# Moving a softmax's sums and scaling from ahead of one elementwise product to behind it, in two chunks of a fused attention and SwiGLU kernel

## The chip, the cores and the metric

The kernel runs on one core of one Trainium2 chip. The metric is the device time of one execution in microseconds (us). One execution was also profiled, and its trace is what the working below is read from. The engines are called as in the profile: PE (TensorE, matmuls; PEld are its weight loads), DVE (VectorE), ACT (ScalarE), POOL (GpSimd) and SP (SyncE, which issues the DMAs).

## The reference

A small set of 32 learned queries `p` packs keys and values of 576 tokens per head; the tokens' queries `q` then attend to the 32 packed rows; a SwiGLU layer follows. There are 8 batch elements, 8 heads, and a head dimension of 64.

```
def sm_attn(qq, kk, vv):
    s = scale * np.matmul(qq, kk.transpose(0, 1, 3, 2))
    s = s - np.max(s, axis=-1, keepdims=True)
    a = np.exp(s)
    a = a / (np.sum(a, axis=-1, keepdims=True) + 1e-09)
    return np.matmul(a, vv)
p_packed = sm_attn(p, k, v)
out = sm_attn(q, p_packed, p_packed)
...
g = x @ w_gate
silu = g * (1.0 / (1.0 + np.exp(-g)))
val = x @ w_val
return (silu * val @ w_out).astype(np.float32)
```

`x` is the attention's output as 4608 tokens of 512 numbers; `w_gate` and `w_val` are 512 by 1536, `w_out` is 1536 by 512. "The second softmax" below is the one of the second `sm_attn`, over 32 packed rows for every token.

## The kernel before

The eight batch elements (called batches, 0 to 7) go through the SwiGLU layer one after the other. Batch 0 follows a written-out list of words; batches 1 to 7 run the loop at L828, and the change touches that loop alone. In it, a batch is twelve **chunks** `fc` = 0 to 11 of 128 hidden units each, and a chunk has two halves of tokens, a (256 wide) and b (320 wide).

For each half, PE computes gate and value into two PSUM banks named `gv` (`gv_chunk`, 6 matmuls each, L558). ACT then takes the SiLU of the gate bank into `sg` (L565), and DVE multiplies it with the value bank into `hf` (L569); in half b a second, narrow product goes into `t4` (L572, shown as `t` in the profile). Products are kept at full precision by splitting each into a high and a low word: ACT copies `hf` to its high word `hh` (L105, in `h_split`), and DVE subtracts to get the low word `hl` (L539). In the following chunk PE multiplies `hl` and `hh` with `w_out` into four accumulators `acc` (`outs`, L577). After every second chunk, 16 further matmuls (`m_part`, L195) prepare the next pair of chunks' weights in two banks named `aux`; ACT copies them to `mh` (L524) and DVE subtracts to get `ml` (L498).

The `gv` pool has two PSUM banks. So the gate matmuls of a half may start when ACT has read the gate bank of the half before, and the value matmuls when DVE has finished both `hf` and `t4` of the half before.

In between these, a batch does the attention of the next batch `d`. `plan_of` says where: `at(fc, place, ...)` puts a step at a place of chunk `fc`. Of a chunk, place "a" lies behind the SiLU of half a, "ha" and "hb" lie between the `hh` copy and the `hl` subtraction of half a and half b, and the numbers 2, 4 and 8 count PE's groups: 2 is behind half a's gate and value matmuls, 4 behind the `outs` that follow (so ahead of half b), 8 at the chunk's end. The second softmax is done in two parts, one in chunks 7 to 9 and one in chunks 9 to 11. Each goes through these steps:

- `s2_mm`: 16 matmuls of scores (L195) into two banks that it takes from the `gv` pool as well (named `gv_aux`), and `s2_block`: two transposes out of them by DVE (L438), at place "ha" of chunk 7 and of chunk 9
- `s2_max`: maximum and subtraction by DVE (L452, L453), at the end of chunk 7 and of chunk 9
- `s2_exp`: exponential by ACT (L457), which needs a table load, and whose next SiLU needs another
- `s2_sums` (L464 to L466) and `s2_scale` (L470): sum, a small addition, reciprocal and a product, by DVE. These are what the change moves
- `s2_turn`: a transpose back by DVE (L479), at the end of chunk 8 and of chunk 10; `s2_high`: ACT's copy to the high word `a2h` (L482); `s2_low`: DVE's low word `a2l` (L486), at place 4 of chunk 9 and of chunk 11

PE's order is the written one. On DVE and ACT the compiler's scheduler settles the order, except that the instructions passed through `pin` keep their written order among each other. Batch 7 has no next batch, so the steps of the plan are run in six batches, 1 to 6.

Of the kernel before, what the change touches and what calls it, by code (L numbers as in the profile page):

```python
# [59 lines left out]
def tile_pack_attention_swiglu(ctx: ExitStack, tc: tile.TileContext, qT, kT, v, vq, pT, wgv, wout, out):  # L60
# [30 lines left out]
    def pin(ins):  # L91

        return tc.keep_in_program_order(ins) if steady[0] else ins
# [71 lines left out]
    def load_k(b):  # L165
        p_t = pool.tile([P, NHP, NP], F32, tag="p", bufs=2, name="p_t")
        (nc.sync if b else nc.scalar).dma_start(p_t, pT[b])
        k_t = io_tile(0, [P, 2, NHP, HS], F32, "k_t")
        if b == 0:
            qs[b] = io_tile(0, [P, 2, NHP, HS], F32, "q_t")  # L170
        for hf in range(2):
            nc.sync.dma_start(k_t[:, hf], kT[b, :, hf])
        kps[b] = (k_t, p_t)
# [135 lines left out]
    def q_scores(b, g, bank=ps):  # L309


        k_t, p_t = kps[b]
        if g == 0:
            e = pool.tile([P, NPAR, NHP, NKQ * NP], F32, tag="s2", bufs=1, name="e1")
            z = pool.tile([P, 2, NPAR, NHP], F32, tag="z1", bufs=2, name="z1")
            sq[b] = [e, z]
            nc.gpsimd.memset(e[:, :, :, SQ:], 0.0)
        e, z = sq[b]
        pss = [bank(), bank()]
        for i in range(2):  # L320
            for j in range(NJ):
                for par in range(NPAR):
                    r = slice(64 * par, 64 * par + 64)
                    nc.tensor.matmul(
                        pss[par][NP * j : NP * j + NP, i * SQ : (i + 1) * SQ],
                        p_t[r, 2 * g + i, :],
                        k_t[r, j // 2, 2 * g + i, j % 2 * SQ : j % 2 * SQ + SQ],
                        start=True, stop=True,
                    )
        sc[b, g] = pss  # L330

    def q_read(b, g, pars):

        e, z = sq[b]
        pss = sc[b, g]
        hs = slice(2 * g, 2 * g + 2)
        for par in pars:
            x, m = pss[par][:, : 2 * SQ].rearrange("p (h n) -> p h n", h=2), z[:, 0, par, hs]
            pin(nc.vector.tensor_reduce(m, x, axis=AX.X, op=ALU.max))
            pin(nc.vector.tensor_tensor(  # L340
                e[:, par, hs, :SQ], x, m.unsqueeze(2).broadcast_to([P, 2, SQ]), op=ALU.subtract
            ))

    def q_exp(b, g):
        x = sq[b][0][:, :, 2 * g : 2 * g + 2, :SQ]
        pin(nc.scalar.activation(x, x, AF.Exp, scale=SCALE))

    def q_sums(b, g):
        e, z = sq[b]
        hs = slice(2 * g, 2 * g + 2)  # L350
        pin(nc.vector.tensor_reduce(z[:, 1, :, hs], e[:, :, hs, :SQ], axis=AX.X, op=ALU.add))

    def q_gather(b):

        x = pool.tile([P, NJ, 2, H], F32, tag="x1", bufs=1, name="x1")
        zd = dram.tile([P, 2, H], F32, tag="zd", bufs=2, name="zd")
        nc.sync.dma_start(zd, sq[b][1].rearrange("p s r h -> p s (r h)"))
        for i in range(NJ):
            nc.sync.dma_start(x[NP * i : NP * i + NP], zd.rearrange("(j n) s h -> n j s h", j=NJ))
        sq[b].append(x)  # L360

    def q_common(b):

        _, z, x = sq[b]
        y = pool.tile([P, 3, NJ + 1, H], F32, tag="pp", bufs=1, name="y1")
        sq[b].append(y)
        m = y[:, 2, 0]
        pin(nc.vector.tensor_reduce(m, x[:, :, 0].rearrange("p j h -> p h j"), axis=AX.X, op=ALU.max))
        pin(nc.vector.tensor_tensor(
            y[:, 0, :NJ], x[:, :, 0], m.unsqueeze(1).broadcast_to([P, NJ, H]), op=ALU.subtract  # L370
        ))
        pin(nc.vector.tensor_tensor(y[:, 0, NJ], z.rearrange("p s r h -> p s (r h)")[:, 0], m, op=ALU.subtract))

    def q_common_exp(b):
        y = sq[b][3]
        pin(nc.scalar.activation(y[:, 0], y[:, 0], AF.Exp, scale=SCALE))

    def q_factors(b):

        _, _, x, y = sq[b]  # L380
        t, f = y[:, 2, 1], y[:, 2, 2]
        pin(nc.vector.tensor_tensor(y[:, 1, :NJ], y[:, 0, :NJ], x[:, :, 1], op=ALU.mult))
        pin(nc.vector.tensor_reduce(t, y[:, 1, :NJ].rearrange("p j h -> p h j"), axis=AX.X, op=ALU.add))
        pin(nc.vector.tensor_scalar(f, t, 1e-9, None, op0=ALU.add))
        pin(nc.vector.reciprocal(t, f))
        pin(nc.vector.tensor_tensor(f, t, y[:, 0, NJ], op=ALU.mult))

    def q_turn(b, par):
        e, f = sq[b][0], sq[b][3][:, 2, 2]
        if par == 0:  # L390
            sq[b].append(pool.tile([P, NPAR, NHP, NKQ, NP], F32, tag="a1", bufs=1, name="a1"))
        w = e[:, par, :, :SQ]
        pin(nc.vector.tensor_tensor(
            w, w, f[:, NHP * par : NHP * par + NHP].unsqueeze(2).broadcast_to([P, NHP, SQ]), op=ALU.mult
        ))
        pin(nc.vector.transpose(
            sq[b][4][:, par].rearrange("p h k n -> p (h k n)"), e[:, par].rearrange("p h n -> p (h n)")
        ))
# [41 lines left out]
    def s2_view(b, cs):  # L440
        s2, r2 = st2[b]
        n = NPAR * NBK
        rows = slice(cs.start * n, cs.stop * n)
        return (
            s2[:, cs].rearrange("p c r (k n) -> p (c r k) n", n=NP),
            [r2[:, i, rows] for i in range(3)],
            [P, (cs.stop - cs.start) * n, NP],
        )
# [13 lines left out]
    def s2_sums(b, cs):  # L462
        x, (m, s, r), _ = s2_view(b, cs)
        pin(nc.vector.tensor_reduce(s, x, axis=AX.X, op=ALU.add))  # L464
        pin(nc.vector.tensor_scalar(m, s, 1e-9, None, op0=ALU.add))
        pin(nc.vector.reciprocal(r, m))  # L466

    def s2_scale(b, cs):
        x, (_, _, r), shape = s2_view(b, cs)
        pin(nc.vector.tensor_tensor(x, x, r.unsqueeze(2).broadcast_to(shape), op=ALU.mult))  # L470
# [121 lines left out]
    def plan_of(b):  # L592

        d, plan = b + 1, {}

        def at(fc, place, *todo):
            plan.setdefault((fc, place), []).extend(todo)  # L600

        if d < B:
            c, c2 = (1, 0) if d % 2 else (0, 1)
            cs, cs2 = slice(c, c + 1), slice(c2, c2 + 1)
            at(0, 2, lambda: q_scores(d, 0))
            at(0, "ha", lambda: q_read(d, 0, (0,)))
            at(0, "hb", lambda: q_read(d, 0, (1,)))
            at(1, "a", lambda: q_exp(d, 0))
            at(1, "ha", lambda: q_scores(d, 1, gv_ps), lambda: q_read(d, 1, (0, 1)))
            at(1, 8, lambda: q_sums(d, 0))  # L610
            at(2, "a", lambda: q_exp(d, 1))
            at(2, 8, lambda: q_sums(d, 1), lambda: q_gather(d))
            at(3, 8, lambda: q_common(d))
            if d + 1 < B:
                at(3, 8, lambda: load_k(d + 1))
            at(4, "a", lambda: q_common_exp(d))
            at(4, 4, lambda: q_factors(d))
            at(4, 8, lambda: q_turn(d, 0))
            at(5, 8, lambda: q_turn(d, 1))
            at(6, 4, lambda: q_pack(d, 0))  # L620
            at(6, 8, lambda: q_pack(d, 1))
            if d + 1 < B:
                at(7, "ha", lambda: load_v(d + 1))
            at(7, "ha", lambda: s2_tiles(d), lambda: s2_a2(d))
            at(7, "ha", lambda: s2_mm(d, c, gv_ps), lambda: s2_block(d, c))
            at(7, 8, lambda: s2_max(d, cs))
            at(8, "a", lambda: s2_exp(d, cs))
            at(8, 4, lambda: s2_sums(d, cs), lambda: s2_scale(d, cs))
            at(8, 8, lambda: s2_turn(d, c), lambda: s2_high(d, c))
            at(9, "ha", lambda: s2_mm(d, c2, gv_ps), lambda: s2_block(d, c2))  # L630
            if d + 1 < B:
                at(9, "ha", lambda: load_q(d + 1))
            at(9, 4, lambda: s2_low(d, c))
            at(9, 8, lambda: s2_max(d, cs2))
            at(10, "a", lambda: s2_exp(d, cs2))
            at(10, 4, lambda: s2_sums(d, cs2), lambda: s2_scale(d, cs2))
            at(10, 8, lambda: s2_turn(d, c2), lambda: s2_high(d, c2))
            at(11, 4, lambda: s2_low(d, c2))
        return lambda fc, place: bool([f() for f in plan.pop((fc, place), ())])

    with tc.manual_schedule(engines={mybir.EngineType.PE}):
# [186 lines left out]
        for b in range(1, B):  # L828
            rows, accs = begin(b)
            run = plan_of(b)  # L830
            ha, hb = {}, {}
# [80 lines left out]
```

## Time and profile before

| what | value |
|---|---|
| time, median of 3 runs (lowest to highest) | 749.33 us (749.03 to 750.16) |
| time of the profiled execution | 749.33 us |
| its span, from the first to the last instruction | 747.5 us |
| busy in the span: PE / DVE / ACT | 736.2 / 455.4 / 367.9 us |
| idle of PE before its `gv` matmuls for `t` of DVE | 1.8 us in 7 waits |
| mean granted PE clock, as a share of full | 0.998 |

The span leaves out 1.8 us of the execution's own time. Busy time of an engine counts overlapping instructions once; PE's matmuls are pipelined, so that one's listed duration reaches into the next ones, and the distance between two starts tells more than a duration. A wait in the profile is idle time of one engine together with the instruction of another engine that ended it.

### The profile page before, as it was taken

The numbers are of one execution on the slowest core, as the hardware profiler recorded it, in microseconds if no ns is written. First come the engines' busy times: TensorE is split into PE (matmuls) and PEld (weight loads), VectorE is DVE, ScalarE is ACT, GpSimd is POOL, SyncE is SP. The second block draws the span as 40 slices with busy tenths as digits, with TensorE's granted clock in tenths as the row PEclk, the third lists the DMA queues.
The fourth block names the chain that finished last, engine by engine and source line by source line (L and its number), as shares of the span: only waits on it lengthen the run. The fifth ranks groups of instructions, "written<-read, shape, count | busy, mean of one in ns | idle before, by whom it ended". The sixth has DMA issues, their size and how long they took to land.

```text
span 747.5 us, 15126 instructions
## 1 busy us (share of the span) xinstructions
PE 736.2 (98%) x6280; PEld 594.8 (80%) x6280; DVE 455.4 (61%) x1004; ACT 367.9 (49%) x662; POOL 2.0 (0%) x13
## 2 busy tenths in 40 slices
PE   7999999999999999999999999999999999999998
PEld 4756666888788887887888888888888888888886
DVE  5988878665756557645765556655575555744334
ACT  3777745754516445563544535464452644533331
POOL 0000000000000000000000000000000000000000
PEclk9999999999999999999999999999999999999999
DMA  9686583202112021302112022100201000010001
GB/s 354 251 313 249 182 323 114 72 3 72 64 71 69 2 72 65 124 4 72 64 57 83 3 72 64 58 3 1 72 2 71 3 1 2 1 57 1 1 1 71
DMA packets 20004, 59.15 MB, mean 79 GB/s; under 512 B 5984, under 2 KB 7008, under 8 KB 17376
## 3 DMA queue, kind: packets, MB, share of 16 engines
q1 hardware_dynamic: 19792, 58.12, 21.5%
q8 instruction: 49, 0.80, 0.5%
q14 instruction: 19, 0.16, 0.1%
q10 hardware_dynamic: 144, 0.07, 0.0%
HBM read 48.69 MB, written 9.49 MB: 78 GB/s over the span
## 4 chain that ended last, share of the span: by engine, by line
PE 90%; DVE 4%; ACT 2%; issue 1%; DVEq 0%; ACTq 0%
PE gv L558 34%; PE acc L577 29%; PE aux L195 7%; PE gv L742 6%; PE acc L768 6%; PE aux L577 4%; PE aux L410 1%; ACT L457 1%; PE gv_aux L195 1%; PE acc L646 1%; DVE hf L569 1%; PE warm_ps L646 1%; DVE hl L539 1%; DVE s L453 1%; ACT hh L105 1%
## 5 line engine op out<-in xcount | busy, mean ns | idle before, releaser
L565 ACT ACTIVATE sg<-gv 128x256 f32<-128x256 f32 (+1 forms) x168 | 68.9, 410 | 166.0 <-PE gv L558 134.7
L558 PE MATMUL gv<-a2h,ml 128*128 128x256 f32 (+1 forms) x672 | 147.2, 300 | 2.3 <-DVE t L572 1.8
L569 DVE TENSOR_TENSOR hf<-gv,sg 128x256 f32<-128x256 f32 x168 | 70.7, 421 | 121.2 <-PE gv L558 99.1
L558 PE MATMUL gv<-a2h,mh 128*128 128x256 f32 (+1 forms) x672 | 144.2, 296 | 0.0
L558 PE MATMUL gv<-a2l,mh 128*128 128x256 f32 (+1 forms) x672 | 144.0, 296 | 0.0
L577 PE MATMUL acc<-wo_h,hl 128*128 128x512 f32 x336 | 136.2, 405 | 0.0
L577 PE MATMUL acc<-wo_l,hh 128*128 128x512 f32 x336 | 132.2, 393 | 0.0
L577 PE MATMUL acc<-wo_h,hh 128*128 128x512 f32 x336 | 131.9, 393 | 0.0
L558 PEld LDWEIGHTS gv<-a2h,ml 128*128 128x128 f32 x672 | 115.1, 189 | 19.3 <-PE gv L558 4.6
L105 ACT CAST hh<-hf 128x256 fp32r<-128x256 f32 x168 | 67.9, 404 | 102.5 <-DVE hf L569 102.4
L539 DVE TENSOR_TENSOR hl<-hf,hh 128x256 fp32r<-128x256 f32 x168 | 70.5, 419 | 78.4 <-ACT hh L105 78.4
L558 PEld LDWEIGHTS gv<-a2h,mh 128*128 128x128 f32 x672 | 108.4, 189 | 0.0
L558 PEld LDWEIGHTS gv<-a2l,mh 128*128 128x128 f32 x672 | 108.1, 189 | 0.0
L577 PEld LDWEIGHTS acc<-wo_h,hl 128*128 128x128 f32 x336 | 63.2, 188 | 34.1 <-issue 26.2
L577 PEld LDWEIGHTS acc<-wo_h,hh 128*128 128x128 f32 x336 | 63.1, 188 | 14.5
L577 PEld LDWEIGHTS acc<-wo_l,hh 128*128 128x128 f32 x336 | 63.2, 188 | 7.9
L498 DVE TENSOR_TENSOR ml<-aux,mh 128x512 fp32r<-128x512 f32 x92 | 59.0, 681 | 4.7 <-ACT mh L524 3.6
L195 PE MATMUL aux<-w,ppt 64*32 64x512 f32 (+1 forms) x784 | 52.4, 588 | 0.5 <-ACT mh L524 0.5
L524 ACT CAST mh<-aux 128x512 fp32r<-128x512 f32 x92 | 49.2, 586 | 4.9 <-PE aux L195 1.9
L565 ACT ACT_TABLE_LOAD x30 | 38.5, 1283 | 16.2 <-PE gv L558 16.1
L768 PE MATMUL acc<-wo_f,h 128*128 128x512 f32 x96 | 44.2, 594 | 0.0
L768 PEld LDWEIGHTS acc<-wo_f,h 128*128 128x128 f32 x96 | 17.3, 189 | 17.2 <-issue 16.5
(149 smaller groups left out, 755.5 us busy)
## 6 DMA issues: line engine op xcount, KB each, us to landing
st<-in_wgv SPq DMA_DIRECT2D x12, 1024.0 KB, 6.4
k_t<-in_kT SPq DMA_DIRECT2D x16, 576.0 KB, 4.8
q_t<-in_qT SPq DMA_DIRECT2D x16, 576.0 KB, 4.9
out<-ot SPq DMA_DIRECT2D x36, 256.0 KB, 2.1
v_t<-in_vq SPq DMA_DIRECT2D x6, 1280.0 KB, 5.5
st<-in_wout SPq DMA_DIRECT2D x6, 1024.0 KB, 5.5
v_t<-in_v SPq DMA_DIRECT2D x2, 1024.0 KB, 8.5
p_t<-in_pT SPq DMA_DIRECT2D x7, 64.0 KB, 2.1
```

What stands on the lines that cost most here:

```text
L105: e.copy(dst, src)
L195: nc.tensor.matmul(outs[par][32 * hp : 32 * hp + 32], lhs(r, hp), rhs(r, hp), start=True, stop=True)
L498: pin(nc.vector.tensor_tensor(*lows.pop(0), op=ALU.subtract))
L524: nc.scalar.copy(m[0][at], src)
L539: low = lo.tensor_tensor(hl, src, hh.bitcast(F32), op=ALU.subtract)
L558: nc.tensor.matmul(pg[:, :n], m_[:, g, f, s * P : (s + 1) * P], a_[:, g, off : off + n], start=(i == 0), stop=(i == 5),)
L565: nc.scalar.activation(sg[:, :n], pgs[0][:, :n], AF.Silu)
L569: nc.vector.tensor_tensor(hf, pgs[1][:, o : o + 256], sg[:, o : o + 256], op=ALU.mult)
L577: nc.tensor.matmul(acc[:, :], h_[:, c : c + P], w_[fc // 2][:, fc % 2], start=(fc == 0 and i == 0), stop=(fc == NFC - 1 and i == 2),)
L646: nc.tensor.matmul(at[:, :P], ident, ident, start=True, stop=True)
L742: nc.tensor.matmul(held[i][s][:, :n], m_[:, g, f, s * P : (s + 1) * P], a_[:, g, off : off + n], start=(j == 0), stop=(j == len(todo) - 1),)
L768: nc.tensor.matmul(accs[2 * is_b + c], half(i)[:, c * P : c * P + P], wos[fc // 2][:, fc % 2], start=(fc == 0), stop=(fc == NFC - 1),)
```

## The change

In chunks 8 and 10, `s2_sums` and `s2_scale` move from place 4 to place "hb". Nothing is added or left out.

```
@@ -625,7 +625,7 @@
             at(8, "a", lambda: s2_exp(d, cs))
-            at(8, 4, lambda: s2_sums(d, cs), lambda: s2_scale(d, cs))
+            at(8, "hb", lambda: s2_sums(d, cs), lambda: s2_scale(d, cs))
             at(8, 8, lambda: s2_turn(d, c), lambda: s2_high(d, c))
...
             at(10, "a", lambda: s2_exp(d, cs2))
-            at(10, 4, lambda: s2_sums(d, cs2), lambda: s2_scale(d, cs2))
+            at(10, "hb", lambda: s2_sums(d, cs2), lambda: s2_scale(d, cs2))
             at(10, 8, lambda: s2_turn(d, c2), lambda: s2_high(d, c2))
```

On DVE, in chunk 8 of batch 4 (the rows begin with `hf` and `hl` of half a; `r` holds sums and reciprocals, `s` the exponentials), the order changes like this:

```order
 L569 TENSOR_TENSOR hf<-gv,sg 128x256
 L539 TENSOR_TENSOR hl<-hf,hh 128x256
+L569 TENSOR_TENSOR hf<-gv,sg 128x256
+L572 TENSOR_TENSOR t_4376<-gv,sg 128x64
 L464 TENSOR_REDUCE r_5015<-s_5014 128x18
 L465 TENSOR_SCALAR r_5015<-r_5015 128x18
 L466 RECIPROCAL r_5015<-r_5015 128x18
 L470 TENSOR_TENSOR s_5014<-s_5014,r_5015 128x576
-L569 TENSOR_TENSOR hf<-gv,sg 128x256
-L572 TENSOR_TENSOR t_4376<-gv,sg 128x64
 L539 TENSOR_TENSOR hl<-hf,hh 128x256
```

Half b's `hf` and `t` now stand ahead of the four instructions of sums and scaling, and half b's `hl` still stands behind them.

What follows on DVE has the same order before and after; in the changed kernel it is this, from half b's `hl` of chunk 8 on (the second `hf` is that of chunk 9's half a, the last one that of its half b):

```order
L539 TENSOR_TENSOR hl<-hf,hh 128x256
L479 STREAM_TRANSPOSE t_5132<-s_5014 128x576
L569 TENSOR_TENSOR hf<-gv,sg 128x256
L438 STREAM_TRANSPOSE s_5014<-gv_aux 128x288 x2
L539 TENSOR_TENSOR hl<-hf,hh 128x256
L498 TENSOR_TENSOR ml<-aux,mh 128x512 x2
L486 TENSOR_TENSOR a2l<-t_5132,a2h 128x2x288
L569 TENSOR_TENSOR hf<-gv,sg 128x256
```

Nothing moved here, but all of it now stands behind sums and scaling with no half of a chunk in between. Chunks 10 and 11 read alike, without the two L438 rows.

On ACT the scheduler also changes one place. In chunk 9 of the same batch, and alike in chunk 11, half a's rows were and are:

```order
 L565 ACTIVATE sg<-gv 128x256
 L482 CAST a2h<-t_5132 128x2x288
-L105 CAST hh<-hf 128x256
-L524 CAST mh<-aux 128x512 x2
+L524 CAST mh<-aux 128x512 x2
+L105 CAST hh<-hf 128x256
 L565 ACTIVATE sg<-gv 128x320
```

Half a's `hh` copy moved behind the two `mh` copies. PE's order is the same in both kernels. Where a batch ends, some copies of finished accumulators (`ot`) change places with a neighbouring `hf`, `hh` or `hl`.

## Rows read from the trace of the kernel before

**Rows 1.** The page: busy time of PE, and the chain that ended last.
```profile
PE 736.2 (98%) x6280; PEld 594.8 (80%) x6280; DVE 455.4 (61%) x1004; ACT 367.9 (49%) x662; POOL 2.0 (0%) x13
...
PE 90%; DVE 4%; ACT 2%; issue 1%; DVEq 0%; ACTq 0%
```

**Rows 2.** Waits, who for whom: us in total, times, longest us.
```profile
PE gv L558 <- DVE t L572: 1.8, 7, 0.4
...
PEld gv_aux L195 <- DVE hf L569: 1.4, 6, 0.2
```

**Rows 3.** Timeline of PE, chunk 9 half a: start, us, engine, what, count, idle before.
```profile
456.73 0.40 PE L558 MATMUL gv<-a2h,mh 128*128 128x256 f32 x2
457.34 0.48 PE L558 MATMUL gv<-a2h,ml 128*128 128x256 f32 x2 [0.22 <-DVE t L572]
...
459.10 0.69 PE L195 MATMUL gv_aux<-q_t,ppt 64*32 64x288 f32 x16
```

**Rows 4.** Timeline of DVE, chunks 8 and 9 of batch 4.
```profile
454.69 0.75 DVE L464 TENSOR_REDUCE r<-s 128x18 f32<-128x576 f32 x1
...
456.65 0.41 DVE L569 TENSOR_TENSOR hf<-gv,sg 128x256 f32<-128x256 f32 x1
456.98 0.21 DVE L572 TENSOR_TENSOR t<-gv,sg 128x64 f32<-128x64 f32 x1
457.53 0.43 DVE L539 TENSOR_TENSOR hl<-hf,hh 128x256 fp32r<-128x256 f32 x1 [0.34 <-ACT hh L105]
457.88 0.77 DVE L479 STREAM_TRANSPOSE t<-s 128x576 f32<-128x576 f32 x1
458.57 0.39 DVE L569 TENSOR_TENSOR hf<-gv,sg 128x256 f32<-128x256 f32 x1
459.88 0.85 DVE L438 STREAM_TRANSPOSE s<-gv_aux 128x288 f32<-128x288 f32 x2 [0.93 <-PE gv_aux L195]
...
463.25 0.42 DVE L569 TENSOR_TENSOR hf<-gv,sg 128x256 f32<-128x256 f32 x1 [0.35 <-PE gv L558]
```

**Rows 5.** Timeline of ACT, chunk 8: the SiLU of half b.
```profile
455.62 0.44 ACT L565 ACTIVATE sg<-gv 128x320 f32<-128x320 f32 x1
```

**Rows 6.** Timeline of ACT, chunks 10 and 11 of batch 4.
```profile
469.59 0.44 ACT L565 ACTIVATE sg<-gv 128x320 f32<-128x320 f32 x1
...
472.38 0.67 ACT L482 CAST a2h<-t 128x576 fp32r<-128x576 f32 x1 [0.71 <-DVE t L479]
472.95 0.40 ACT L105 CAST hh<-hf 128x256 fp32r<-128x256 f32 x1
473.26 1.06 ACT L524 CAST mh<-aux 128x512 fp32r<-128x512 f32 x2
```

**Rows 7.** Timeline of DVE, chunk 11 of batch 4.
```profile
472.26 0.39 DVE L569 TENSOR_TENSOR hf<-gv,sg 128x256 f32<-128x256 f32 x1
473.39 0.42 DVE L539 TENSOR_TENSOR hl<-hf,hh 128x256 fp32r<-128x256 f32 x1 [0.73 <-ACT hh L105]
473.87 1.29 DVE L498 TENSOR_TENSOR ml<-aux,mh 128x512 fp32r<-128x512 f32 x2
475.07 0.75 DVE L486 TENSOR_TENSOR a2l<-t,a2h 128x576 fp32r<-128x576 f32 x1
476.45 0.42 DVE L569 TENSOR_TENSOR hf<-gv,sg 128x256 f32<-128x256 f32 x1 [0.63 <-PE gv L558]
...
477.35 0.43 DVE L539 TENSOR_TENSOR hl<-hf,hh 128x256 fp32r<-128x256 f32 x1 [0.34 <-ACT hh L105]
```

**Rows 8.** Timeline of PE, end of batch 4: neighbours at half b's first `hl` matmul.
```profile
478.73 0.39 PE L577 MATMUL acc<-wo_h,hh 128*128 128x512 f32 x1
478.96 0.40 PE L577 MATMUL acc<-wo_h,hl 128*128 128x512 f32 x1
```

**Rows 9.** Windows: stretch, length, busy by engine, granted PE clock, DMA share, GB/s.
```profile
14.00:17.00 3.00, 1.61 (x41) 0.61 (x48) 2.59 (x5) 0.40 (x2) 0.00 (x0) 0.99 1.04 429
17.00:20.00 3.00, 3.00 (x25) 2.08 (x26) 2.88 (x6) 1.60 (x4) 0.00 (x0) 0.50 0.95 320
...
456.25:464.36 8.11, 7.89 (x69) 6.10 (x69) 6.15 (x15) 3.48 (x8) 0.00 (x0) 1.00 0.38 97
```

More of the change, by code (lines that the diff above doesn't have):

```diff
@@ L627, in plan_of @@
             at(8, "a", lambda: s2_exp(d, cs))
-            at(8, 4, lambda: s2_sums(d, cs), lambda: s2_scale(d, cs))
+            at(8, "hb", lambda: s2_sums(d, cs), lambda: s2_scale(d, cs))
             at(8, 8, lambda: s2_turn(d, c), lambda: s2_high(d, c))
@@ L635, in plan_of @@
             at(10, "a", lambda: s2_exp(d, cs2))
-            at(10, 4, lambda: s2_sums(d, cs2), lambda: s2_scale(d, cs2))
+            at(10, "hb", lambda: s2_sums(d, cs2), lambda: s2_scale(d, cs2))
             at(10, 8, lambda: s2_turn(d, c2), lambda: s2_high(d, c2))
```

## The prediction

> **What bounds the kernel now.** I read the page first: PE is busy 98% of the span and the chain that ended last runs 90% over PE [rows 1]. So a move on DVE costs or gains nothing by its own length; it counts only where PE waits for DVE or ACT. I therefore read the waits next, for PE and its weight loads. Two small lines touch the moved code [rows 2]. The first: PE's `gv` matmuls wait for `t`, the last reader of a value bank, 7 times, 1.8 us in total. The second: the weight loads of the `gv_aux` scores wait for `hf`, 6 times, 0.2 us at most; the scores take over the bank that this `hf` reads.
>
> The timelines show where they lie. In chunk 9 of batch 4 half a's value matmuls start at 457.34 [rows 3]. The last gate pair starts at 456.73, and a pair takes 0.24 us of PE here (0.40 is latency), so the start was due at 456.97: PE lost 0.37 us. On DVE, chunk 8's half b had its SiLU ready at 455.62 + 0.44 = 456.06 [rows 5], but `hf` began at 456.65, when the four sums-and-scale instructions, begun at 454.69, were out of the way [rows 4]. In six batches this is 6 x 0.37 = 2.2 us. Chunk 11, behind the same group in chunk 10, has no such wait.
>
> Thirdly, chunk 9's half-a `hf` runs from 458.57 to 458.96 and the scores' matmuls start at 459.10, 0.14 us later [rows 3, 4]. That is the tight spot: the scores have almost no slack against this `hf`, in each of the six batches.
>
> **The change, step by step.** *What it gives.* With the group gone from in front, chunk 8's half-b `hf` starts right behind its SiLU: 456.06 plus 0.04 of hand-over (an `hh` copy ends at 473.35, its `hl` starts at 473.39 [rows 6, 7]) = 456.10. `t` follows 0.33 us on [rows 4], at 456.43, and ends at 456.64, before PE wants the bank at 456.97. The 0.37 us vanish.
>
> *What it costs in chunk 9.* Behind `t` now come, without a break, the group, `hl`, the transpose and then `hf` of chunk 9. Their start-to-start distances [rows 4]: `t` to the next 0.13 to 0.21 (its duration is 0.21, and `hl` and transpose overlap by 0.08), the group 456.65 - 454.69 = 1.96, `hl` 457.88 - 457.53 = 0.35, the transpose 458.57 - 457.88 = 0.69. So the group starts at 456.56 to 456.64, `hl` at 458.52 to 458.60, the transpose at 458.87 to 458.95, chunk 9's `hf` at 459.56 to 459.64. It ends 0.39 later, at 459.95 to 460.03, where before it ended at 458.96. `hl` no longer waits for `hh` (0.34 idle before), which is counted, since the chain has no idle in it.
>
> PE meanwhile arrives 0.37 earlier, at 458.73, and its next work is the scores. They can start at 459.95 to 460.03 plus the 0.14 seen before, that is 460.09 to 460.17, against 459.10. If the 0.14 was partly PE's own pace, it is 0.05 at the least, and the start 460.00. So PE comes out of chunk 9 later by 0.9 to 1.07 us; I take 1.0. The recovered 0.37 is inside this, spent on the longer wait. PE's order is fixed, so nothing steps in for the scores. Times six: **6.0 us**.
>
> The rest of chunk 9 follows PE's new pace: the scores' transposes, `ml` and `a2l` come ahead of half b's `hf`, which PE would allow at 463.25 + 1.0 = 464.25 [rows 4]. `a2h` waits for the late transpose (ends 459.72 at most), `hh` now stands behind the `mh` pair, and with chunk 11's distances below `hh` ends at about 461.8. `hl`, two `ml` and `a2l` then fill DVE until about 464.0: in time, with 0.25 us to spare. Nothing added here.
>
> *What it costs in chunk 11.* Times stay those of before; PE's delay shifts both sides alike. Chunk 10's half-b SiLU ends at 469.59 + 0.44 = 470.03 [rows 6], `hf` starts at 470.07, and by the same distances the group starts at 470.53 to 470.61, `hl` at 472.49 to 472.57, the transpose at 472.84 to 472.92, chunk 11's `hf` at 473.53 to 473.61, against 472.26 [rows 7]. There are no scores in chunk 11, so PE does not wait here. But ACT does: `a2h` starts when the 0.77 us transpose ends, at 473.65 to 473.73 instead of 472.38 [rows 6]. The next copy may start 0.57 later, two `mh` take 1.06 less an overlap of 0.08, and only then comes `hh`, at 475.20 to 475.28, where it was at 472.95. `hl` follows 0.44 later, at 475.64 to 475.72, the `ml` pair 0.35 on, `a2l` 1.20 on, half b's `hf` 0.67 on: 477.86 to 477.94 against 476.45 [rows 7]. Its `hl` comes 477.35 - 476.45 = 0.90 later, at 478.76 to 478.84, and ends 0.43 on, at 479.19 to 479.27. PE wants it for the batch's last group at 478.96, and loads it as weights one step earlier, at 478.73 [rows 8]. The matmul then starts 0.05 to 0.23 behind the end of `hl`: 479.24 to 479.50, so 0.28 to 0.54 late. I take 0.45. Times six: **2.7 us**. Were DVE's chain 0.3 shorter than I make it, this wait would be nothing.
>
> *What costs nothing.* The `ot` copies that change places at the batches' ends: the next reader of their banks is a chunk away. POOL clears a tile that waits for the same transpose, 1.3 us later now, but still within chunk 11, and the tile's first use is in the next batch. No DMA moves.
>
> *A rule on DVE weighed.* In the rows an instruction that waits for nothing starts 0.08 us before its forerunner ends: `hl` runs until 457.96, the transpose starts at 457.88 [rows 4]. The Trainium skill, page "VectorE: DVE Perf Modes", section "The DRAIN you can't avoid", says that the next operation does not start until the previous one's pipeline has emptied. By that, the sum would be that of rival E, 13.5 us instead of 8.7. These rows contradict it for these operations, so I stay with their distances.
>
> **The sum.** 6 x 1.0 + 6 x 0.45 = 8.7 us. The profiled execution took 749.33 us, which is also the median: 749.33 + 8.7 = **758.0 us**, slower.
>
> **The rivals.** *(A) Only the scores wait.* If ACT's and DVE's queues in chunk 11 run 0.3 us or more ahead of my working, only chunk 9 pays: 749.33 + 6.0 = 755.3 us. For it: that chain is the longest that I add up, ten instructions. Against: `hh` behind the `mh` pair is in the program's order.
>
> *(B) The wait is only removed, and the kernel gets faster.* Then 749.33 - 2.2 = 747.1 us. For it: the wait for `t` is real and its cause is moved away. The place that decides is chunk 9's `hf`. To keep the gain whole it must end by 458.73 - 0.14 = 458.59, that is start at 458.20, 2.1 us behind the half-b `hf`, where the chain needs 3.46 to 3.54. Even to lose nothing it must start at 458.57 as before, and the chain must be 1.0 us shorter. Only a group half as long, or scores in other banks, would do that; nothing in the rows speaks for it.
>
> *(C) No change within the measurement's reach.* The gain of 0.37 and a wait of about that size would have to cancel, with the chain some 0.9 to 1.2 us shorter than by rows. Time: 749.3 us.
>
> *(D) The idle stretches bring PE's clock down.* It has happened in this trace: from 14 to 17 us PE was busy 1.61 of 3.00 us, and from 17 to 20 its granted clock was 0.50, the 1.2 GHz level [rows 9]. A 3 us stretch at that level loses up to 1.5 us; one in each batch makes 758.0 + 9.0 = 767 us. Against: chunk 9 with its wait is at 1.00 [rows 9], and a batch's new idle, about 1.4 us, is parted over two places 20 us from each other [rows 3, 8]. The page "TensorE: Matmul & The Clock Gate" of the Trainium skill, Part 1, has this as a rule: activity releases the throttle and idleness brings it back. The trace agrees that it can.
>
> *(E) DVE's instructions don't overlap behind the moved group.* The five overlaps of 0.08 in my chain go, chunk 9's `hf` comes 0.4 us later still, and with the like in chunk 11 the sum is 8.7 + 6 x 0.8 = 13.5 us: 762.8 us. Against: the same pairs overlap in the rows of before. The DRAIN rule above would have it so.
>
> **How the numbers follow.** The forecast 0.72 (756 to 760 us), A 0.13, B 0.04, C 0.03, D 0.03, E 0.02, and 0.03 for waits that I overlooked, mostly beyond 760. The range has to hold 8 in 10: the bounds give 6 x (0.9 + 0.28) = 7.1 and 6 x (1.07 + 0.54) = 9.7 us, so 756.4 to 759.0; taking in A, whose lower bound is 749.33 + 5.4 = 754.7, and something above for a chain that carries further, I give 754.7 to 760.2. A difference of 0.2% is what a measurement of this kernel can tell from no change. Faster 0.04 (B), the same 0.04 (C and a little of A), slower 0.92.
>
> **What would show it.** The waits of PE for `t` before `gv` fall from 7 to 1. The scores in `gv_aux` wait for `hf` six times, by about 1.0 us or a little more each. Chunk 9's half-a `hf` starts about 3.5 us behind chunk 8's half-b `hf`, instead of 1.92. At the six batch ends PE waits for `hl` before `acc`, by some 0.4 us. Chunk 8 keeps its length. I am wrong if DVE idles between half b's `t` and chunk 9's `hf`, if the scores start before that `hf` ends, or if the granted clock is under 1.00 after them.

## The result

| | before | after |
|---|---|---|
| median of 6 runs each (lowest to highest) | 749.75 us (748.65 to 751.39) | 756.87 us (755.67 to 758.18) |
| the profiled execution, its span | 749.33 us, 747.5 us | 757.44 us, 755.7 us |
| mean granted PE clock of the profiled execution | 0.998 | 0.998 |

The ratio is 1.0095, 95% interval 1.0082 to 1.0109: about 7.1 us (6.1 to 8.2) slower. Forecast were 758.0 us and 8.7 us; the range of 754.7 to 760.2 holds the time. Of the executions of all kernels below, one, of the kernel with only chunk 10 moved, took 1830 us and is left out of its ratio.

The page of the changed kernel: PE's busy share is what it was, 98%, and the chain that ended last now runs more over DVE and ACT (11% and 7%, from 4% and 2% in [rows 1]).

```profile
PE 739.7 (98%) x6280; PEld 593.0 (78%) x6280; DVE 453.5 (60%) x1004; ACT 367.6 (49%) x662; POOL 2.0 (0%) x13
...
PE 74%; DVE 11%; ACT 7%; DMA 4%; issue 1%; SPq 0%; ACTq 0%; DVEq 0%
```

The waits of the changed kernel (who for whom: us in total, times, longest us) answer to [rows 2]. The 7 waits of `gv` for `t` are gone. The weight loads of the scores wait 7.4 us for `hf` instead of 1.4, PE itself waits 4.2 us there, and a new wait for `hl` stands at the batches' ends, six times.

```profile
PEld gv_aux L195 <- DVE hf L569: 7.4, 6, 1.2
...
PE gv_aux L195 <- DVE hf L569: 4.2, 6, 0.7
...
PEld acc L577 <- DVE hl L539: 3.4, 6, 0.6
```

The timeline of DVE in chunks 8 and 9 of batch 4, against [rows 4]:

```profile
458.64 0.42 DVE L539 TENSOR_TENSOR hl<-hf,hh 128x256 fp32r<-128x256 f32 x1 [1.93 <-ACT hh L105]
460.39 0.42 DVE L569 TENSOR_TENSOR hf<-gv,sg 128x256 f32<-128x256 f32 x1 [1.32 <-ACT sg L565]
460.73 0.22 DVE L572 TENSOR_TENSOR t<-gv,sg 128x64 f32<-128x64 f32 x1
460.86 0.74 DVE L464 TENSOR_REDUCE r<-s 128x18 f32<-128x576 f32 x1
...
462.15 0.76 DVE L470 TENSOR_TENSOR s<-s,r 128x576 f32<-128x576 f32 x1
462.82 0.42 DVE L539 TENSOR_TENSOR hl<-hf,hh 128x256 fp32r<-128x256 f32 x1
463.16 0.77 DVE L479 STREAM_TRANSPOSE t<-s 128x576 f32<-128x576 f32 x1
463.85 0.39 DVE L569 TENSOR_TENSOR hf<-gv,sg 128x256 f32<-128x256 f32 x1
```

Read it from the second row. Half b's `hf` now starts when its SiLU is done; in front of it DVE idles 1.32 us, where sums and scaling used to lie. Then come seven instructions with no wait between them that the view lists, and chunk 9's `hf` starts 463.85 - 460.39 = 3.46 us later, where it was 1.92. PE at the same place, against [rows 3]:

```profile
462.95 0.65 PE L195 MATMUL gv_aux<-q_t,ppt 64*32 64x288 f32 x2
464.29 0.71 PE L195 MATMUL gv_aux<-q_t,ppt 64*32 64x288 f32 x14 [0.70 <-DVE hf L569]
464.94 0.50 PE L577 MATMUL acc<-wo_h,hl 128*128 128x512 f32 x1
```

PE reaches the scores at 462.95. In the program they go to their two banks by turns (`by_head`, L190). The first two records are for the bank that the SiLU had read, and they start. What comes next is for the bank that `hf` reads, and as PE keeps its order, all other 14 records stand until 464.29, also those for the free bank. That is 0.05 us after `hf` ends at 463.85 + 0.39 = 464.24. The gap is 1.34 us from start to start.

The other wait begins on ACT and ends on PE. First ACT in chunk 11 of batch 4, against [rows 6]:

```profile
478.84 0.67 ACT L482 CAST a2h<-t 128x576 fp32r<-128x576 f32 x1 [1.97 <-DVE t L479]
479.42 1.07 ACT L524 CAST mh<-aux 128x512 fp32r<-128x512 f32 x2
480.37 0.42 ACT L105 CAST hh<-hf 128x256 fp32r<-128x256 f32 x1
```

ACT stands 1.97 us until the late transpose frees `a2h`; both `mh` copies and then `hh` queue behind it. On DVE, against [rows 7], the delay goes on from `hl` through `ml` and `a2l` to half b's `hf`, with no wait between them, and from there to the last `hl`:

```profile
478.73 0.38 DVE L569 TENSOR_TENSOR hf<-gv,sg 128x256 f32<-128x256 f32 x1
480.82 0.42 DVE L539 TENSOR_TENSOR hl<-hf,hh 128x256 fp32r<-128x256 f32 x1 [1.71 <-ACT hh L105]
481.16 1.28 DVE L498 TENSOR_TENSOR ml<-aux,mh 128x512 fp32r<-128x512 f32 x2
482.36 0.75 DVE L486 TENSOR_TENSOR a2l<-t,a2h 128x576 fp32r<-128x576 f32 x1
483.03 0.42 DVE L569 TENSOR_TENSOR hf<-gv,sg 128x256 f32<-128x256 f32 x1
...
483.92 0.42 DVE L539 TENSOR_TENSOR hl<-hf,hh 128x256 fp32r<-128x256 f32 x1 [0.34 <-ACT hh L105]
```

PE at the end of the batch, against [rows 8]:

```profile
483.87 0.40 PE L577 MATMUL acc<-wo_h,hh 128*128 128x512 f32 x1
484.40 0.50 PE L577 MATMUL acc<-wo_h,hl 128*128 128x512 f32 x1
484.74 0.39 PE L577 MATMUL acc<-wo_l,hh 128*128 128x512 f32 x1
```

The matmul with `hl` comes 0.53 us behind its forerunner, and the next 0.34 us behind it, where PE's pace is 0.23 [rows 8]: 0.41 us lost.

The windows of chunk 9 and chunk 11 of batch 4 (stretch, length, busy time of PE, PEld, DVE, ACT, POOL, granted clock, DMA share, GB/s), chunk 9 to set against [rows 9]:

```profile
460.54:469.56 9.02, 8.32 (x69) 6.08 (x69) 7.50 (x18) 3.58 (x8) 0.00 (x0) 1.00 0.34 96
475.52:485.89 10.37, 10.23 (x65) 7.87 (x64) 7.27 (x17) 4.07 (x9) 0.20 (x1) 1.00 0.02 4
```

Chunk 9 grew from 8.11 to 9.02 us; chunk 11 was 10.04 us before (470.32 to 480.36). The granted clock stayed at 1.00, the 2.4 GHz level, in both. The other five batches show the same in the two traces: chunk 9 is 0.90 to 0.93 us longer, chunk 11 0.29 to 0.34 us.

### The profile page after: what moved, and what is told of

Same layout as the page of the kernel before. It is cut to its first block, busy times and chain, and to the rows that moved or that the text cites. A ratio compares the mean times of both kernels' runs of the same rounds, so it can differ in the third digit from the quotient of the medians.

```text
span 755.7 us, 15126 instructions
## 1 busy us (share of the span) xinstructions
PE 739.7 (98%) x6280; PEld 593.0 (78%) x6280; DVE 453.5 (60%) x1004; ACT 367.6 (49%) x662; POOL 2.0 (0%) x13
## 4 chain that ended last, share of the span: by engine, by line
PE 74%; DVE 11%; ACT 7%; DMA 4%; issue 1%; SPq 0%; ACTq 0%; DVEq 0%
PE gv L558 29%; PE acc L577 24%; PE aux L195 5%; PE aux L577 4%; PE gv L742 4%; PE acc L768 4%; DMA st<-in_wout 3%; ACT L565 2%; DVE hf L569 2%; PE gv_aux L195 1%; PE aux L410 1%; DVE t L479 1%; DVE s L470 1%; DVE hl L539 1%; DVE r L464 1%
## 5 line engine op out<-in xcount | busy, mean ns | idle before, releaser
L569 DVE TENSOR_TENSOR hf<-gv,sg 128x256 f32<-128x256 f32 x168 | 70.8, 421 | 140.9 <-PE gv L558 101.2
```

Of the source, the lines that this page charges most:

```text
L569: nc.vector.tensor_tensor(hf, pgs[1][:, o : o + 256], sg[:, o : o + 256], op=ALU.mult)
```

## The experiments

The table gives for each kernel the length of chunks 9 and 11 in batch 4 (from the first `gv` matmul of a chunk to that of the next, by the trace) and the result. "Over before" is the ratio less one, times the median of before in the same comparison: 749.75 us for the changed kernel, 749.18 us for the run with `hf` held and the two with a late transpose, 749.09 us for the others. It can differ by up to 0.6 us from the difference of the medians.

| kernel | chunk 9 | chunk 11 | median | ratio, 95% interval | over before |
|---|---|---|---|---|---|
| before | 8.11 | 10.04 | | | |
| after | 9.02 | 10.37 | 756.87 | 1.0095 (1.0082 to 1.0109) | +7.1 |
| only chunk 8 moved | 9.02 | 10.05 | 754.36 | 1.0066 (1.0054 to 1.0078) | +4.9 |
| only chunk 10 moved | 8.12 | 10.36 | 751.33 | 1.0033 (1.0019 to 1.0047) | +2.5 |
| group split | 7.74 | 9.98 | 746.73 | 0.9967 (0.9956 to 0.9978) | -2.5 |
| sum twice | 8.05 | 10.37 | 750.23 | 1.0012 (1.0004 to 1.0021) | +0.9 |
| sum twice, `hf` held | 9.81 | 10.38 | 761.16 | 1.0156 (1.0133 to 1.0178) | +11.7 |
| chunk 8's transpose late | 8.36 | 9.97 | 749.94 | 1.0005 (0.9995 to 1.0015) | +0.4 |
| chunk 10's transpose late | 9.05 | 9.98 | 754.08 | 1.0057 (1.0036 to 1.0078) | +4.3 |

The theory is that of the forecast: chunk 9's scores wait for `hf`, and the batch's last group waits for `hl`, and nothing else counts. The rivals are named with each run.

**One move without the other.** Each of the two lines of the change alone.

```
-            at(8, 4, lambda: s2_sums(d, cs), lambda: s2_scale(d, cs))
+            at(8, "hb", lambda: s2_sums(d, cs), lambda: s2_scale(d, cs))
```

> Only chunk 8's sums and scaling moved; chunk 10's stay at place 4. My theory (chunk 9's scores wait for a late hf, by 0.91 us net in each of six batches; chunk 11's last hl, by 0.33 us) expects 6 x 0.91 = 5.5 us over before, chunk 9 at 9.0 us and chunk 11 as before, no wait of PE for hl. Rival, that each of the two moved groups costs about alike: 3.6 us. Rival, that the loss comes with the accumulator copies that change places at the batches' ends (they keep their places here): no loss, or a gain of 2.2 us from the wait for t that goes.

The same in chunk 10 alone:

```
-            at(10, 4, lambda: s2_sums(d, cs2), lambda: s2_scale(d, cs2))
+            at(10, "hb", lambda: s2_sums(d, cs2), lambda: s2_scale(d, cs2))
```

> Only chunk 10's sums and scaling moved; chunk 8's stay at place 4. My theory expects 6 x 0.33 = 2.0 us over before: chunk 9 stays at 8.1 us with its 0.37 us wait for t, and PE waits for hl before the last group of six batches. Rival, that each moved group costs alike: 3.6 us. Rival of the accumulator copies: the whole 7 us.

Chunk 8's move cost 4.9 us (4.0 to 5.8; the theory's 5.5 lies inside), with the wait of the scores as in the changed kernel and none for `hl`; chunk 10's cost 2.5 us (1.4 to 3.5, with the theory's 2.0), with the wait for `hl` alone, which its trace has as in the changed kernel:

```profile
PEld acc L577 <- DVE hl L539: 3.4, 6, 0.6
```

Together 7.4 us, the whole loss within the intervals. The rival of equal shares (3.6 us each) falls: 3.6 us is outside the first interval and just outside the second. So does the one of the accumulator copies: they keep their places in the first run, which has most of the loss.

**The group split.** Sums and reciprocal back at place 4, the scaling behind half b's `hf`, in both chunks.

```
-            at(8, "hb", lambda: s2_sums(d, cs), lambda: s2_scale(d, cs))
+            at(8, 4, lambda: s2_sums(d, cs))
+            at(8, "hb", lambda: s2_scale(d, cs))
```

> The group is split in chunks 8 and 10: sums and reciprocal stay at place 4, only the scaling product moves to hb. My theory: sums and reciprocal take 1.28 us of the old 1.96, end at the time the SiLU is ready, so that half b's hf starts on time (the 0.37 us wait for t goes), and the chain behind hf is 1.28 us shorter than in the changed kernel, so chunk 9's hf ends at or before its old time and the scores don't wait: chunk 9 at 7.75 to 7.8 us, 2.0 to 2.2 us under before (747.6). A rival, that any of this work behind half b's hf delays PE: 1 to 3 us over before. A rival, that the wait for t is not worth its length: same as before within 0.5 us.

2.5 us under before: the version that beats both kernels. DVE in chunk 8 of batch 4:

```profile
452.61 0.43 DVE L539 TENSOR_TENSOR hl<-hf,hh 128x256 fp32r<-128x256 f32 x1 [1.93 <-ACT hh L105]
452.95 0.74 DVE L464 TENSOR_REDUCE r<-s 128x18 f32<-128x576 f32 x1
453.73 0.18 DVE L465 TENSOR_SCALAR r<-r 128x18 f32<-128x18 f32 x1
453.94 0.27 DVE L466 RECIPROCAL r<-r 128x18 f32<-128x18 f32 x1
454.36 0.42 DVE L569 TENSOR_TENSOR hf<-gv,sg 128x256 f32<-128x256 f32 x1 [0.15 <-ACT sg L565]
454.70 0.21 DVE L572 TENSOR_TENSOR t<-gv,sg 128x64 f32<-128x64 f32 x1
454.83 0.75 DVE L470 TENSOR_TENSOR s<-s,r 128x576 f32<-128x576 f32 x1
455.49 0.42 DVE L539 TENSOR_TENSOR hl<-hf,hh 128x256 fp32r<-128x256 f32 x1
455.83 0.77 DVE L479 STREAM_TRANSPOSE t<-s 128x576 f32<-128x576 f32 x1
456.52 0.38 DVE L569 TENSOR_TENSOR hf<-gv,sg 128x256 f32<-128x256 f32 x1
```

Sums and reciprocal fit in front of the SiLU (0.15 us of idle is left), and chunk 9's `hf` comes 456.52 - 454.36 = 2.16 us behind half b's, instead of 3.46. Chunk 9 is 7.74 us, and the list of waits has none of PE or its weight loads for this `hf` or for chunk 8's `t`.

**The sum twice.** The changed kernel with chunk 8's sum taken a second time.

```
-            at(8, "hb", lambda: s2_sums(d, cs), lambda: s2_scale(d, cs))
+            at(8, "hb", lambda: s2_sums(d, cs, 2), lambda: s2_scale(d, cs))
```

> The changed kernel with the sum of chunk 8 taken twice (0.75 us more DVE work in six batches, same output). The scheduler then puts chunk 9's half-a hf ahead of the small addition, the reciprocal, the scaling and the transpose, right behind the second sum. My theory (only the time of that hf counts for the scores): hf ends before PE reaches the scores, no wait for hf, chunk 9 at 7.8 us; with chunk 11's 0.33 us left, 750 us less 2.2 plus 2.0: within 0.7 us of before and about 7 us under the changed kernel, although DVE does 4.5 us more. The rival, that DVE's work behind half b is what PE pays for: up to 4.5 us over the changed kernel, some 761 us.

More work in the same place and 6 us less time than the changed kernel: 0.9 us over before. Chunk 9's `hf` now comes at 459.17, ahead of reciprocal and scaling, and no wait for it is left:

```profile
457.25 0.43 DVE L570 TENSOR_TENSOR hf<-gv,sg 128x256 f32<-128x256 f32 x1 [1.32 <-ACT sg L566]
457.59 0.21 DVE L573 TENSOR_TENSOR t<-gv,sg 128x64 f32<-128x64 f32 x1
457.72 1.53 DVE L465 TENSOR_REDUCE r<-s 128x18 f32<-128x576 f32 x2
459.17 0.41 DVE L570 TENSOR_TENSOR hf<-gv,sg 128x256 f32<-128x256 f32 x1
```

The size was off: chunk 9 is 8.05 us, not 7.8. A wait that I had not counted stands in it. The scores' transposes (L438) are now behind the pushed-back scaling and transpose, and half b's `gv` takes over the banks that they read:

```profile
PEld gv L559 <- DVE s L438: 3.2, 6, 0.5
```

The same instructions with that one product held in the changed kernel's order:

```
+        if fc == 9 and not is_b:
+            pin(mul)
```

(`mul` is the `hf` product of L569.)

> The run with the sum of chunk 8 taken twice, again, but with chunk 9's half-a hf held in the changed kernel's order, behind the scaling, half b's hl and the transpose. The same instructions as in that run; only the place of this one product differs. My theory: the second sum's 0.78 us (start to start) goes into PE's wait for hf one to one, chunk 9 at 9.02 + 0.78 = 9.8 us, 6 x 0.78 = 4.7 us over the changed kernel, about 12 us over before. A rival, that PE's wait depends on other things than this product's place and the order made no difference: as in that run, about 1 us over before.

Chunk 9 is 9.81 us, 0.79 over the changed kernel's for a second sum of 0.74 us and the gap behind it, and the run is 11.7 us over before (10.0 to 13.3; the theory said about 12). From half b's `hf` to chunk 9's it is now 465.86 - 461.60 = 4.26 us. The two products and the waits of the scores:

```profile
461.60 0.42 DVE L570 TENSOR_TENSOR hf<-gv,sg 128x256 f32<-128x256 f32 x1 [1.33 <-ACT sg L566]
...
465.86 0.39 DVE L570 TENSOR_TENSOR hf<-gv,sg 128x256 f32<-128x256 f32 x1
```

```profile
PEld gv_aux L195 <- DVE hf L570: 12.1, 6, 2.0
```

Between these two runs only the order differs: on DVE, in these chunks, this product alone has another place, and on ACT half a's `hh` follows it to behind `mh` and `a2h`. That is 10.9 us by the medians. DVE's amount of work is not what PE pays for.

**The transpose late.** The changed kernel with `s2_turn` and `s2_high` of chunk 8 moved into chunk 9, behind the scores' transposes.

```
-            at(8, 8, lambda: s2_turn(d, c), lambda: s2_high(d, c))
             at(9, "ha", lambda: s2_mm(d, c2, gv_ps), lambda: s2_block(d, c2))
+            at(9, "ha", lambda: s2_turn(d, c), lambda: s2_high(d, c))
```

> The changed kernel with chunk 8's transpose back and its high-word copy moved into chunk 9, behind the scores' transposes. The chain in front of chunk 9's half-a hf loses the transpose's 0.69 us. My theory: chunk 9 at 9.02 - 0.69 = 8.33 us, 0.22 over before; in chunk 11 the scheduler's order now has the half-a hf ahead of the scaling and hh ahead of the mh copies, so that no wait for hl is left: 6 x 0.22 = 1.3 us over before. A rival, that the four moved instructions alone make the loss and the transpose is covered: 5.5 us over before.

Chunk 9 fell by 0.66 us to 8.36, nearly the transpose's 0.69, and a shorter wait is left:

```profile
PEld gv_aux L195 <- DVE hf L569: 3.5, 6, 0.6
```

Measured were 0.4 us over before, with an interval of -0.4 to +1.1: the 1.3 expected lie just outside. Chunk 11 came out 0.07 us under before, which the expectation had at nothing; by the chunks' lengths six batches are 6 x (0.25 - 0.07) = 1.1 us over. Of the 6.7 us or so that this run gains on the changed kernel, 6 x 0.66 = 4.0 are chunk 9's. Another 6 x 0.40 = 2.4 are chunk 11's, where the scheduler also put half a's `hf` ahead of the scaling and `hh` ahead of the `mh` copies. The transpose, not part of the change, is a fifth of the chain that the change makes late.

The same with chunk 10's transpose, moved to place "ha" of chunk 11:

```
-            at(10, 8, lambda: s2_turn(d, c2), lambda: s2_high(d, c2))
+            at(11, "ha", lambda: s2_turn(d, c2), lambda: s2_high(d, c2))
```

> The changed kernel with chunk 10's transpose back and its high-word copy moved into chunk 11, behind half a's hf; the hh copy then stands ahead of the two mh copies and of a2h on ACT. My theory (the wait for hl at a batch's end comes from hh standing behind a late a2h and two mh): no wait of PE for hl, chunk 11 as before at 10.04 and 18.40 us, chunk 9 still at 9.02, 5.5 us over before. The rival, that chunk 11's loss comes from the four moved instructions in chunk 10 whatever ACT's order: 7.4 us over before.

No wait for `hl` is left and chunk 11 is 9.98 us, though sums and scaling of chunk 10 stay moved. The time, 4.3 us over before (2.7 to 5.8), is nearer to the theory's 5.5 than to the rival's 7.4, which lies outside. ACT in chunk 11, which starts at 473.38 in this run:

```profile
476.34 0.41 ACT L105 CAST hh<-hf 128x256 fp32r<-128x256 f32 x1 [1.61 <-DVE hf L569]
476.65 1.07 ACT L524 CAST mh<-aux 128x512 fp32r<-128x512 f32 x2
477.61 0.69 ACT L482 CAST a2h<-t 128x576 fp32r<-128x576 f32 x1
```

`a2h` starts 4.23 us into the chunk, later than the 478.84 - 475.52 = 3.32 of the changed kernel, and nothing is lost. So a late `a2h` does no harm where `hh` and the `mh` copies stand ahead of it. This run moves two things at once, `hh` on ACT and half a's `hf` ahead of the transpose on DVE, and no run takes them apart. An estimate from rows: with ACT's old order half b's `hf` came 475.07 + 0.67 - 472.38 = 3.36 us behind the start of `a2h` [rows 6, 7] (0.67 is the distance from `a2l`'s start to `hf`'s, 483.03 - 482.36). In the changed kernel it came 483.03 - 478.84 = 4.19 us behind. The old order alone would have brought it 0.83 us earlier, more than the 0.30 us by which the matmul with `hl` came late. So by this estimate ACT's order alone makes the difference between a wait and none; no run shows it.

## Why the prediction was right

- **What it gives.** Right: half b's `hf` follows its SiLU, and the wait for `t` is gone (one wait outside the moved chunks was to stay; this execution has none, the run with only chunk 8 moved lists one of 0.4 us). The gain was a little more than the 0.37 us forecast: PE reaches the scores 462.95 - 460.54 = 2.41 us into chunk 9, where it was 459.10 - 456.25 = 2.85 [rows 3, 9], 0.44 us sooner. The longer wait behind it takes all of this up, as forecast. The sentence that chunk 11 has no such wait was wrong in the small: in the trace of before the first pair of its half-a value matmuls took 0.32 us instead of 0.24, and in the changed kernel the place keeps its pace. That is 6 x 0.07 = 0.4 us of gain by the length of chunk 11's first part (4.10 to 4.03 us), not in the sum. The pair in the trace of before:

```profile
471.03 0.47 PE L558 MATMUL gv<-a2h,ml 128*128 128x256 f32 x2
471.35 0.40 PE L558 MATMUL gv<-a2l,mh 128*128 128x256 f32 x2
```

- **Chunk 9.** Right in mechanism and place. The chain was forecast at 3.46 to 3.54 us and is 3.46: `t` to the next took the low bound, 0.13. The term was forecast as 1.0 us and measured 9.02 - 8.11 = 0.91. The step that was mis-sized is the hand-over from `hf` to the scores: I took the 0.14 us of before, where PE came at its own pace, and the wait shows 0.05, which the forecast had as its lower bound without a row for it. The weight load of before shows it, at 459.01, 0.05 us behind the end of `hf` at 458.96 [rows 4]:

```profile
459.01 0.24 PEld L195 LDWEIGHTS gv_aux<-q_t,ppt 64*32 64x32 f32 x15 [0.23 <-DVE hf L569]
```
- **A sign of being wrong that came up.** The forecast named as one that the scores start before that `hf` ends. By the letter they do: two of the 16 records start at 462.95, and `hf` ends at 464.24. The forecast had overlooked that the first of them need the other bank. The sum does not change by it, because the next record needs the bank that `hf` reads, and the rest stands behind it.
- **Chunk 11.** Right: `a2h`, two `mh`, `hh`, then DVE's queue up to the last `hl`. Forecast 0.45, the wait cost 0.41. That it came so near is in part luck: the matmul itself was 0.53 - 0.23 = 0.30 us late, at the lower end of the forecast's 0.28 to 0.54, and the other 0.11 is the slow step behind it, which the forecast had not counted. With the 0.07 that the chunk got back, 10.37 - 10.04 = 0.33 is left.
- **The sum.** 6 x 0.91 + 6 x 0.33 = 7.4 us by the trace of batch 4, against 8.7 forecast and 7.1 measured. The profiled executions differ by 8.1 us; what goes beyond 7.4 lies outside chunks 9 and 11 (the first chunk of batch 1 starts 0.46 us later).
- **What costs nothing.** Chunk 9's remainder kept its pace: half b takes 3.14 us as before. The accumulator copies cost nothing that shows; the run without their changes, chunk 8's move alone, keeps its share of the loss.
- **The rivals.** A needed no wait in chunk 11: there are six. B and C needed a shorter chain behind half b's `hf`; the split run is B come true, with a chain of 2.16 us, about the 2.1 that the forecast named, and gained 2.5 us against B's 2.2. D: the granted clock stayed at 1.00 around the new waits. E: the overlaps on DVE are as they were; `hl` at 462.82 lasts 0.42 and the transpose starts at 463.16, 0.08 us before its end. The forecast took only half of what the Trainium skill says on the page "VectorE: DVE Perf Modes", section "The DRAIN you can't avoid": the section adds that a next op which is not held starts earlier. Read whole, it leaves room for these overlaps, and the rows do not contradict it; whether these instructions count as held was not worked out here.

## What to carry to other kernels

When work is moved off the path of one result, follow the queue that it joins up to the next result that the busy engine wants there: here 0.44 us of PE's time was won by one product, and 1.34 us lost at the next, 3.5 us further on. Ask there which bank each matmul wants: one late bank held up all the scores behind it, also those for the free bank. An order of the scores that fills the free bank first was not run. Look for the idle time in front of the product first, and fill it with as much of the work as fits: splitting the group gained where moving it whole lost. Where a scheduler sets part of the order, read the order that it makes: one more instruction changed it, and with it the time by nearly as much as the change itself did.

## What the runs showed of the hardware

PE's gap at the scores, 1.34 us from start to start, left the granted clock of the chunk at 1.00. The window of the run with the sum twice and `hf` held says the same from the start of batch 1 into the last chunk of batch 6 (columns as in [rows 9]), though its weight loads stood up to 2.0 us:

```profile
126.00:664.00 538.00, 527.77 (x4796) 437.90 (x4795) 316.37 (x747) 261.08 (x478) 1.04 (x5) 1.00 0.13 45
```

After the wait for `hl`, the first step of PE was slower than its pace: 0.34 us to the next matmul instead of 0.23.
